# Linear attention and a channel mix on one core: batch 4 turned to tokens on partitions, all steps in a new order, 14 zero matmuls in front, the last tile in three pieces

## The chip, the core and the metric

The kernel runs on 1 core of one Trainium2 chip. The metric is the device time of one execution in microseconds (us): 198.37 us, the median of 3 runs (198.21 to 198.51). One more execution was taken with the profiler and is told apart below. The engines are TensorE (PE; its weight loads are PEld), VectorE (DVE), ScalarE (ACT), GpSimd (POOL) and SyncE (SP). POOL and SP issue the DMA transfers here.

## What is computed

```python
kv = np.einsum('bhsd,bhse->bhde', k, v)          # q, k, v: 8 batches, 8 heads, 576 tokens, 64
out = np.einsum('bhsd,bhde->bhse', q, kv)
rms = np.sqrt(np.mean(out * out, axis=-1, keepdims=True) + 1e-06)
x = (out / rms * g_norm)                         # then heads side by side: 8 x 576 x 512
x_prev = x shifted by one token, zero in front
xk = mu_k * x + (1 - mu_k) * x_prev              # xr likewise with mu_r
k = np.maximum(xk @ w_k, 0.0)                    # 512 -> 1024
v = k * k @ w_v                                  # 1024 -> 512
r = 1.0 / (1.0 + np.exp(-(xr @ w_r)))            # 512 -> 512
return r * v
```

Inputs and output are float32; the matmuls are in bfloat16.

## The kernel before

All eight batches are worked off in a pipeline. Nothing is scheduled by a compiler: ORDER (lines 18 to 109) is a list of words, and a loop at the end of the kernel issues one step for each word. `K.3.1.0=5` is step K of batch 3, part 1, half 0, into PSUM bank 5; a `'` at the end sends the step to VectorE instead of ScalarE. Each engine and each DMA queue gets its steps in the order of this list and works them off strictly in that order; semaphores make a step wait for its inputs and for a free buffer. A step at the head of a queue that waits holds up all behind it on that queue, and nothing on the others. So a place in the list says what a step is behind, and not when it runs.

**A batch a goes through these steps.** `ld.0.a`, `ld.1.a`, `ld.2.a` (line 201) load k, v and q on POOL's queue, with a cast to bfloat16. There are 3 buffers for k, 3 for v, 2 for q. `kv.a` (line 328) multiplies k and v on PE, 72 small matmuls into two banks; `kvo` copies them out. `qd.a.0` and `qd.a.1` (line 359) turn q on the DMA engines, issued by SP, into qT and qTr. `gt.a` (line 365) is a gate: POOL copies one column of qT, and so the loads listed behind it on POOL start only when qT has landed. Then u = q times kv in one of two forms:

- *Channels on partitions* (`u`, line 368): 24 matmuls of 64 x 64. `sq` squares on ScalarE, `ms` (line 436) averages over a head on PE by a matmul with a constant matrix, `rs` takes the reciprocal root on ScalarE, `mu` (line 448) scales on VectorE and writes xT. There are five pieces n = 0 to 4; the fifth holds the 64 tokens that are left over.
- *Tokens on partitions* (`ut`, line 386): 16 matmuls of 128 x 128 in four steps. `sqt` squares on ScalarE, `rdt` sums over a head on VectorE, `rst` takes the root of a small tile on ScalarE, `mut` scales on VectorE into y, `yd` (line 418) turns y into xT on the DMA engines, issued by SP, and `gs` (line 422) multiplies by g_norm on VectorE. Only the left-over 64 tokens go by `ur` (line 394) and one `sq`, `ms`, `rs`, `mu`; `kvr` (line 352) makes the operand of `ur`.

Before the change batches 2, 3 and 4 use the first form and 5, 6 and 7 the second; batches 0 and 1 have steps of their own at the start (`kc`, `qc`, `uc`, `Kf`, `Kl`).

With xT there, `d` (line 484) takes differences of neighbouring tokens, `sc` and `add` (lines 495, 508) blend them into xr (first index 1) and xk (0). `R` (line 572, 4 matmuls of 512 columns) and `S` make the sigmoid, `K` (line 552, 4 matmuls of 288 columns) is xk @ w_k, `Ko` its relu, `ks` its square, `V` (line 582, two halves of 4 matmuls) is the product with w_v. `fin` (line 597) multiplies V by the sigmoid into an out_sb tile (9 buffers) and `st` (line 613) stores it on SP's queue. A tile t of R and V has 128 tokens of a pair of batches, 0 to 8; t = 4 has 64 of each.

At the start `wm` (line 249) runs matmuls on zeros. The last tile is done apart: `L`, `Lf`, `Ls` (lines 588, 597, 619) in two column halves, each stored in two halves of 64 partitions, one on SP's queue and one on ScalarE's.

SP's queue has, between the start and the stage of batch 5, this order of transposes and stores (a store word of batches 0 and 1 is two transfers): qd.2.0, qd.3.0, qd.2.1, st.0.3, qd.3.1, st.0.0, st.0.1, qd.4.0, st.0.2, qd.4.1, st.1.5, st.1.6, qd.5.0, st.1.7, qd.5.1, st.1.8, st.2.1, st.1.4, qd.6.0, yd.5.0, yd.5.1, yd.5.3, yd.5.2, st.3.4, st.2.0, qd.7.0. POOL's queue has: (first loads), gt.2, gt.3, v3, k3, v4, k4, v5, q4, k5, gt.4, k6, q5, v6, gt.5, v7, k7, q6, q7, gt.6.

Of the kernel before, what the change touches and what calls it, by code (L numbers as in the profile page):

```python
# [18 lines left out]
    set.0 set.2 lraw.1 lraw.0 lrow wm.12=0 lf.0.2.0.2.0.576 lf.0.2.2.4.0.576 lf.0.0.2.3.0.576 lf.0.1.2.3.0.576  # L19
    set.1 wm.7=1 col.0=1 cast.1 cast.0' qc.0.0.2.192.576=23 qco.0.1.192.576 kc.0.0.2=45 kco.0.1 kco.0.0' wm.2=6  # L20
    uc.0.1=6 qc.0.2.4.0.192=70 qco.0.2.0.192' qco.0.3.0.192' qc.0.2.4.192.576=34 qco.0.0.192.576 sq.0.1 uc.0.0=5
    sq.0.0 col.1 qco.0.2.192.576' ms.0.1=2 rs.0.1 mu.0.1 qc.0.0.2.0.192=70 qco.0.0.0.192 ms.0.0=1 rs.0.0 mu.0.0
    kc.0.2.3=3 kco.0.2 wm.2=2 uc.0.2=2 sq.0.2 qco.0.3.192.576 lf.0.1.3.4.0.576 dc.0.0.2.256.576 lf.0.0.3.4.0.576
    kc.0.3.4=7 kco.0.3 wm.1=1 ms.0.2=1 rs.0.2 wm.1=6 uc.0.3=6 sq.0.3 uc.0.4=3 sq.0.4 sc.0.0.0.256.576'
    sc.0.0.1.256.576' qco.0.1.0.192' wm.1=5 uc.0.6=5 sq.0.6 add.0.0.0.256.576 mu.0.2 ms.0.3=4 rs.0.3 mu.0.3
    ms.0.4=7 rs.0.4 mu.0.4 wrap.0 uc.0.5=0 sq.0.5 ms.0.6=1 rs.0.6 dc.0.2.3.256.576 lf.1.2.0.4.0.576 wm.2=2
    qc.1.0.2.0.576=24 qco.1.1.0.576 qc.1.2.4.0.576=76 qco.1.3.0.576 fu.0.0.2.256.576 mu.0.6 dc.0.3.4.256.576
    ms.0.5=3 rs.0.5 qco.1.2.0.576 tab.1.0 fu.0.0.3.256.576 mu.0.5 dc.0.0.4.0.256 sc.0.0.0.0.256 sc.0.0.1.0.256
    lw.0.0.0.4.0.2 Kf.1.0.2.256=1 Kf.0.0.2.256=4 Kf.0.2.3.256 qco.1.0.0.576' lw.0.1.0.4.2.4 wm.2=6
    Kf.3.0.2.256=6 Kf.2.0.2.256=5 Kf.2.2.3.256 Kf.2.3.4.256 Kf.3.2.3.256 Kf.3.3.4.256 sc.0.1.0' sc.0.1.1'  # L30
# [24 lines left out]
    zl Ko.2.2.0' Ko.2.0.1' u.3.1=06 sq.3.2 sq.3.3 K.2.3.0=4 ks.2.0 K.2.1.0=3 Ko.2.3.0' st.1.6 K.2.5.1=7
    Ko.2.5.0' ms.3.3=1 K.2.1.1=5 rs.3.3 Ko.2.5.1' ms.3.2=4 rs.3.2 Ko.2.1.0' Ko.2.1.1' mu.3.2 ld.0.6 K.2.2.1=2
    ks.2.1 Ko.2.2.1 ld.2.5 u.3.2=7 kv.4=31 u.3.0=54 K.2.3.1=0 mu.3.3 K.2.6.1=2 kvo.4.3' ld.1.6 sq.3.4 kvo.4.2'
    qd.5.0 gt.5 kvo.4.0' sq.3.0 ms.3.0=6 sq.3.1 kvo.4.1' Ko.2.3.1 ks.2.5' rs.3.0 ks.2.2' K.2.7.1=1 ms.3.1=3
    rs.3.1 K.2.7.0=0 Ko.2.7.0 Ko.2.7.1' mu.3.0 K.2.4.1=6 K.2.6.0=1 ks.2.3' kvo.4.5 ks.2.7 mu.3.1 ms.3.4=3 rs.3.4
    Ko.2.6.0 K.2.4.0=0 Ko.2.4.0' Ko.2.4.1 ks.2.4 Ko.2.6.1 ks.2.6 d.3.0 d.3.4 mu.3.4 V.2.0.0=5 d.3.1 d.3.2  # L60
    V.2.3.0=4 sc.3.0.0' sc.3.1.0 sc.3.1.2 st.1.7 V.2.1.0=3 V.2.1.1 qd.5.1 kvo.4.4 sc.3.1.3' sc.3.0.3' sc.3.1.1
    sc.3.0.2 fin.2.1 st.1.8 st.2.1 add.3.1.1 V.2.0.1 fin.2.0 V.2.3.1 kv.5=10 kvo.5.3 kvo.5.0 u.4.1=62 u.4.0=73
    kvo.5.2 st.1.4 add.3.1.0 tab.1.3 R.3.7=5 sc.3.0.1' fin.2.3 kvo.5.1 R.3.6=0 S.3.6 sq.4.1 R.3.5=4 S.3.5 sq.4.2
    S.3.7 add.3.0.0 ld.1.7 ld.0.7 ld.2.6 R.3.4=1 S.3.4 add.3.0.1 K.3.3.0=0 R.3.8=4 S.3.8 tab.0.4 Ko.3.3.0'
    K.3.3.1=5 Ko.3.3.1' K.3.5.0=0 K.3.5.1=1 Ko.3.5.0' Ko.3.5.1' ms.4.1=4 rs.4.1 K.3.1.0=5 K.3.2.0=0 Ko.3.2.0'
    Ko.3.1.0 K.3.7.0=1 Ko.3.7.0' K.3.7.1=4 Ko.3.7.1' sq.4.3 sq.4.0 ms.4.2=5 rs.4.2 K.3.2.1=0 ms.4.3=1 K.3.6.0=4
    K.3.6.1=5 mu.4.1 Ko.3.2.1' ks.3.2' rs.4.3 mu.4.3 K.3.1.1=3 kvo.5.4 Ko.3.6.0' Ko.3.6.1 ks.3.6' Ko.3.1.1
    ks.3.7 ms.4.0=0 ld.2.7 K.3.4.0=1 mu.4.2 K.3.0.0=5 Ko.3.0.0 ks.3.1' ks.3.3 K.3.0.1=2 Ko.3.0.1 ks.3.0' rs.4.0
    mu.4.0 kvr.5.1' u.4.2=3 kv.6=45 kvo.6.3' sq.4.4 V.2.2.0=6 ks.3.5 Ko.3.4.0 V.2.2.1 d.4.0 kvo.5.5 fin.2.2
    ms.4.4=2 K.3.4.1=0 rs.4.4 mu.4.4 d.4.4 Ko.3.4.1 kvo.6.0 d.4.1 d.4.2 ks.3.4 d.4.3 sc.4.1.0 sc.4.0.0'  # L70
    V.3.6.0=7 sc.4.1.3' V.3.7.0=1 qd.6.0 gt.6 V.3.7.1 sc.4.1.1' fin.3.7 add.4.1.0 sc.4.1.2 sc.4.0.1 add.4.1.1
    kvo.6.1 V.3.5.0=2 ut.5.1=0 add.4.0.0 sc.4.0.2 V.3.6.1 fin.3.6 V.3.5.1 tab.1.4 sc.4.0.3' fin.3.5 R.4.1=6
    S.4.1 add.4.0.1 R.4.3=3 kvo.6.5 ut.5.0=1 sqt.5.0 rdt.5.0 kvr.6.0' R.4.0=4 S.4.0 S.4.3 sqt.5.1 rdt.5.1
    K.4.3.0=7 R.4.2=6 S.4.2 kvo.6.2 K.4.5.0=2 K.4.3.1=4 Ko.4.3.0' K.4.4.0=3 Ko.4.3.1' tab.0.5 kvr.5.0 Ko.4.5.0'
    ut.5.2=6 sqt.5.2 Ko.4.4.0' rst.5.0 mut.5.0 mut.5.1 yd.5.0 yd.5.1 K.4.5.1=5 K.4.2.0=7 rdt.5.2 kv.7=42
    ut.5.3=3 kvo.7.2' Ko.4.5.1 sqt.5.3 rdt.5.3 Ko.4.2.0 kvo.7.3 K.4.6.0=5 Ko.4.6.0' V.3.4.0=1 ks.4.3 rst.5.1
    mut.5.2 kvo.7.1 kvo.6.4 mut.5.3 K.4.4.1=0 V.3.4.1 fin.3.4 K.4.1.1=7 ur.5=2 kvr.6.1 Ko.4.4.1 sq.5.4 K.4.7.1=5
    K.4.7.0=6 K.4.2.1=0 Ko.4.7.0 ms.5.4=3 Ko.4.7.1 rs.5.4 Ko.4.2.1' mu.5.4 K.4.1.0=1 K.4.0.0=6 Ko.4.0.0
    K.4.0.1=5 ut.6.0=0 kvo.7.0' ks.4.5 Ko.4.0.1 ks.4.2 ks.4.0 sqt.6.0 Ko.4.1.0' ks.4.4 Ko.4.1.1' ks.4.1'
    K.4.6.1=3 Ko.4.6.1 ks.4.7' yd.5.3 gs.5.1 V.3.8.0=2 V.3.8.1 fin.3.8 ut.6.2=4 ks.4.6 V.4.1.0=6 ut.6.1=1  # L80
# [32 lines left out]
def kernel(  # L113
# [605 lines left out]
```

## Time and profile before

| | |
|---|---|
| runs shown | 198.37, 198.51, 198.21 us; median 198.37 |
| profiled execution, its own time | 198.81 us |
| its span, first to last instruction | 197.0 us |
| granted TensorE clock | 1.00 |
| last matmul starts and ends (line 593) | 191.13 for all 16; 193.06 us |
| kv.3, kv.4, kv.5, kv.6, kv.7 start on PE (line 337) | 66.75, 74.0, 84.57, 98.4, 114.04 us |

The profile page gives the busy time of each engine, then the span in 40 slices of 4.9 us, in which a digit is the busy share in tenths. The chain of waits gives who waited for whom. In a timeline the columns are start, duration, engine and line, operation, out<-in, count; the bracket holds the idle time before and what ended it. An answer on DMA issues gives the transfers issued in a window, the KB that each writes, and the median time from issue to landing. In a group of instructions the mean is that of one instruction; matmuls overlap, so the time that one takes on PE is read from a run of them: 64 K matmuls in 7.84 us (0.490 for a K), 20 V matmuls in 4.32 (0.864 for four), 16 R in 3.45, 72 kv in 0.71.

### The profile page before, as it was taken

The page shows a single profiled execution, that of the slowest core. Times are in us where ns is not written, and L with a number is a line of the kernel's source. Part 1 is how long each engine was busy: PE and PEld are TensorE (multiplying, and loading weights), DVE is VectorE, ACT ScalarE, POOL GpSimd, SP SyncE. Part 2 cuts the span into 40 slices and gives each one's busy share as a digit, 9 for nine tenths or more (in the row PEclk, how much of TensorE's full clock was granted, in tenths as well). Part 3 has the DMA queues.
Part 4 walks back from the last instruction along what each step waited for, and adds up shares of the span by engine and source line. Part 5 has one row for each costly group of instructions (what it writes and reads, how often), then busy time and mean ns, then how long its engine had stood idle before and what let it go on. Part 6 is the DMA issues. An engine that isn't in the chain of part 4 may idle for free.

```text
span 197.0 us, 4744 instructions
## 1 busy us (share of the span) xinstructions
PE 189.2 (96%) x1879; PEld 111.4 (57%) x1900; DVE 150.0 (76%) x331; ACT 153.4 (78%) x297; POOL 33.2 (17%) x54
## 2 busy tenths in 40 slices
PE   7989999999999999999999999999999999999991
PEld 2445754447744566456754667546854586476451
DVE  4177957894998778984989778897897898779141
ACT  3389799887688799999998978998699877267810
POOL 7864431000390000520090000000000000000000
PEclk9999999999999999999999999999999999999999
DMA  6999999999699999899979995982530426006053
GB/s 218 214 204 197 204 206 207 206 193 198 116 172 232 207 201 168 178 220 201 189 122 245 194 198 106 200 260 89 130 101 0 161 53 194 25 0 237 32 160 106
DMA packets 49035, 32.24 MB, mean 164 GB/s; under 512 B 25324, under 2 KB 44020, under 8 KB 49012
## 3 DMA queue, kind: packets, MB, share of 16 engines
q0 software_dynamic: 22160, 16.19, 54.9%
q1 hardware_dynamic: 26692, 15.61, 32.9%
q8 instruction: 15, 0.25, 0.5%
q10 hardware_dynamic: 160, 0.13, 0.3%
q14 instruction: 8, 0.07, 0.1%
HBM read 33.56 MB, written 9.44 MB: 218 GB/s over the span
## 4 chain that ended last, share of the span: by engine, by line
PE 85%; DVE 6%; ACT 6%; issue 1%; ACTq 0%
PE ps_v L585 28%; PE ps_km L555 24%; PE ps_r L575 15%; PE ps_warm L252 4%; PE ps_ms L438 3%; PE ps_km L530 2%; DVE xT L462 2%; PE ps_km L541 1%; PE ps_u L391 1%; PE ps_u L323 1%; ACT sq L434 1%; ACT L647 1%; ACT sig L580 1%; PE ps_kv L337 1%; PE ps_v L593 1%
## 5 line engine op out<-in xcount | busy, mean ns | idle before, releaser
L585 PE MATMUL ps_v<-wv_sb,sqk 128*128 128x512 bf16 x269 | 63.1, 379 | 0.5
L555 PE MATMUL ps_km<-xk,wk_sb 128*128 128x288 bf16 x448 | 61.0, 286 | 0.0
L555 PEld LDWEIGHTS <-wk_sb 128*128 128x128 bf16 x448 | 42.9, 98 | 14.7 <-issue 1.0
L585 PEld LDWEIGHTS <-sqk 128*128 128x128 bf16 x280 | 27.0, 98 | 30.5 <-ACT sqk L523 1.2
L519 DVE TENSOR_SCALAR rt<-ps_km 128x288 bf16<-128x288 f32 (+2 forms) x61 | 26.4, 460 | 10.1 <-PE ps_km L555 8.8
L575 PE MATMUL ps_r<-wr_sb,xr 128*128 128x512 bf16 x137 | 32.8, 379 | 0.5 <-DVE m L501 0.2
L600 DVE TENSOR_TENSOR out_sb<-ps_v,sig 128x512 f32<-128x512 f32 (+1 forms) x37 | 24.6, 671 | 10.0 <-PE ps_v L585 4.4
L517 ACT ACTIVATE rt<-ps_km 128x288 bf16<-128x288 f32 (+2 forms) x63 | 24.6, 419 | 8.8 <-PE ps_km L555 7.0
L499 ACT ACTIVATE m<-dx,cols 128x576 bf16<-128x576 bf16 (+1 forms) x32 | 22.4, 750 | 4.6 <-DVE dx L490 2.9
L580 ACT ACTIVATE sig<-ps_r 128x512 bf16<-128x512 f32 x36 | 20.7, 607 | 4.9 <-PE ps_r L575 4.6
L523 ACT ACTIVATE sqk<-rt 128x576 bf16<-128x576 bf16 (+1 forms) x33 | 22.3, 691 | 1.6 <-DVE rt L519 1.4
L575 PEld LDWEIGHTS <-xr 128*128 128x128 bf16 x144 | 14.0, 98 | 15.5 <-DVE xr L510 0.2
L462 DVE SCALAR_TENSOR_TENSOR xT<-ps_u,cols,rs 128x512 bf16<-128x512 f32 (+4 forms) x31 | 19.0, 626 | 3.7 <-ACT rs L443 3.4
L443 ACT ACTIVATE rs<-ps_ms,eps 128x512 f32<-128x512 f32 (+4 forms) x31 | 18.0, 593 | 3.9 <-PE ps_ms L438 3.6
L647 ACT ACT_TABLE_LOAD x15 | 19.2, 1283 | 0.3
L434 ACT ACTIVATE sq<-ps_u 128x512 bf16<-128x512 f32 (+4 forms) x31 | 14.6, 502 | 1.1 <-PE ps_u L323 1.0
L525 DVE TENSOR_TENSOR sqk<-rt 128x576 bf16<-128x576 bf16 (+2 forms) x27 | 12.9, 491 | 2.8 <-ACT rt L517 2.3
L366 POOL COPY gates<-qT 128x1 bf16<-128x1 bf16 x5 | 1.5, 305 | 74.1 <-DMA qT<-in_q 74.1
L510 DVE TENSOR_TENSOR xr<-m,xT 128x1152 bf16<-128x1152 bf16 x16 | 11.6, 752 | 1.6 <-ACT m L499 1.5
L510 DVE TENSOR_TENSOR xk<-m,xT 128x1152 bf16<-128x1152 bf16 (+2 forms) x17 | 11.7, 698 | 0.6 <-ACT m L499 0.5
L252 PE MATMUL ps_warm<-zeros 128*128 128x512 bf16 x27 | 10.0, 503 | 1.4 <-DVE eps L259 1.2
L501 DVE TENSOR_SCALAR m<-dx,cols 128x576 bf16<-128x576 bf16 (+2 forms) x34 | 10.9, 358 | 0.2
(80 smaller groups left out, 172.3 us busy)
## 6 DMA issues: line engine op xcount, KB each, us to landing
out_dram<-out_sb SPq DMA_DIRECT2D x23, 256.0 KB, 2.8
in_k<-in_k_dram POOLq DMA_DIRECT2D x7, 576.0 KB, 13.9
in_v<-in_v_dram POOLq DMA_DIRECT2D x6, 576.0 KB, 11.7
in_q<-in_q_dram POOLq DMA_DIRECT2D x6, 512.0 KB, 16.2
out_dram<-out_sb SPq DMA_DIRECT2D x24, 128.0 KB, 2.8
wk_sb<-in_moe_w_k_dram POOLq DMA_DIRECT2D x4, 256.0 KB, 10.6
wv_sb<-in_moe_w_v_dram POOLq DMA_DIRECT2D x2, 512.0 KB, 15.1
sqk<-in_v_dram SPq DMA_DIRECT2D x1, 576.0 KB, 3.7
```

The lines of the kernel that those rows point to most:

```text
L462: DVE.scalar_tensor_tensor(out=dst, in0=ps, scalar=g_sb, in1=rs, op0=ALU.mult, op1=ALU.mult)
L499: eng.activation(out=out_, in_=in_, func=AF.Copy, scale=mu)
L510: DVE.tensor_add(out=blended(a, which)[:, hs, c0:c1], in0=at[a]["m", which][:, hs, c0:c1], in1=xT[a % 2][:, hs, P + c0:P + c1])
L517: eng.activation(out=dst, in_=ps, func=AF.Relu)
L519: eng.tensor_scalar(out=dst, in0=ps, scalar1=0.0, scalar2=None, op0=ALU.max)
L523: eng.activation(out=dst, in_=src, func=AF.Square)
L555: nc.tensor.matmul(ps, wk_sb[:, cc, 128 * fc:128 * fc + 128], at[b]["xk"][:, cc, SH * h:SH * h + SH], start=(cc == 0), stop=(cc == NHP - 1))
L575: nc.tensor.matmul(ps, xr[:, cc, 128 * t:128 * t + 128], wr_sb[:, cc, :], start=(cc == 0), stop=(cc == NHP - 1))
L580: ACT.activation(out=sig[b, t], in_=give(("r", b, t)), func=AF.Sigmoid)
L585: nc.tensor.matmul(ps, sqk[:, fc, 128 * t:128 * t + 128], wv_sb[:, fc, :], start=(fc == 0), stop=(fc == NFC - 1))
L600: DVE.tensor_mul(out=o, in0=give(("v",) + key), in1=sig[b, t][:, c])
L647: "tab": lambda eng, n, b: ACT.preload_act_table_set(("abs_reciprocal_sqrt_and_small", "sigmoid_and_others")[n]),
```

## The change

ORDER is a new list throughout. Of the steps themselves:

- Batch 4 goes from `u` to `ut`: out go u.4.0 to u.4.2, four each of sq, ms, rs and mu; in come ut, sqt, rdt, mut and yd of 4.0 to 4.3, two each of rst, kvr and gs, and ur.4.
- The zero matmuls are 14 in front (12 and 7 before, around a wait for the small rows) and 27 in all instead of 30; kc.0 now stands ahead of the first qc.
- The last tile is done in pieces of 256, 128 and 128 columns, each stored by one transfer of 128 partitions: the first on SP, the second on ScalarE's queue, the third on SP.
- Some evacuations change between ScalarE and VectorE (Ko 55 and 57 before, 60 and 52 after; ks 32 and 24 before, 29 and 27 after).

SP's queue in the same stretch: qd.2.0, qd.3.0, qd.2.1, qd.3.1, st.0.2, st.0.0, st.0.1, qd.4.0, st.0.3, qd.4.1, st.1.5, st.1.7, qd.5.0, yd.4.1, yd.4.2, yd.4.3, yd.4.0, qd.6.0, st.1.6, qd.5.1, st.1.4, st.2.2, yd.5.1, yd.5.0, yd.5.3, yd.5.2, st.2.0, st.1.8, qd.7.0. POOL's queue: (first loads), gt.2, gt.3, v3, k3, v5, v4, k4, q4, k5, gt.4, k6, v6, q5, q6, gt.5, gt.6, k7, v7, q7. On PE, kv.6 now stands ahead of most of K.3, and kv.7 behind nine steps of K.4.

The diff, cut to what is spoken of:

```diff
-    set.0 set.2 lraw.1 lraw.0 lrow wm.12=0 lf.0.2.0.2.0.576 lf.0.2.2.4.0.576 lf.0.0.2.3.0.576 lf.0.1.2.3.0.576
-    set.1 wm.7=1 col.0=1 cast.1 cast.0' qc.0.0.2.192.576=23 qco.0.1.192.576 kc.0.0.2=45 kco.0.1 kco.0.0' wm.2=6
...
-    S.3.7 add.3.0.0 ld.1.7 ld.0.7 ld.2.6 R.3.4=1 S.3.4 add.3.0.1 K.3.3.0=0 R.3.8=4 S.3.8 tab.0.4 Ko.3.3.0'
...
-    mu.4.0 kvr.5.1' u.4.2=3 kv.6=45 kvo.6.3' sq.4.4 V.2.2.0=6 ks.3.5 Ko.3.4.0 V.2.2.1 d.4.0 kvo.5.5 fin.2.2
...
-    V.3.6.0=7 sc.4.1.3' V.3.7.0=1 qd.6.0 gt.6 V.3.7.1 sc.4.1.1' fin.3.7 add.4.1.0 sc.4.1.2 sc.4.0.1 add.4.1.1
...
-    ut.5.2=6 sqt.5.2 Ko.4.4.0' rst.5.0 mut.5.0 mut.5.1 yd.5.0 yd.5.1 K.4.5.1=5 K.4.2.0=7 rdt.5.2 kv.7=42
...
-    S.7.5 fin.7.5 st.7.5 fin.7.6 st.7.6 L.1=7 Lf.1 Ls.0.1 Ls.1.1 L.0=4 Lf.0 Ls.0.0 Ls.1.0
...
+    set.0 set.2 lraw.1 lraw.0 lrow wm.14=0 lf.0.2.0.2.0.576 lf.0.2.2.4.0.576 lf.0.0.2.3.0.576 lf.0.1.2.3.0.576
+    set.1 cast.1 cast.0' kc.0.0.2=12 kco.0.0 qc.0.0.2.0.192=34 qco.0.1.0.192' kco.0.1' qc.0.0.2.192.576=56
...
+    sqt.4.3 fin.2.0 sc.3.0.1 R.3.7=2 V.2.3.1 S.3.7 qd.5.0 ut.4.1=0 gt.5 R.3.6=3 sqt.4.1 kvo.5.5' kvr.4.0
...
+    tab.0.4 rst.4.0 K.3.4.0=2 Ko.3.4.0' ut.4.2=3 K.3.4.1=6 Ko.3.4.1' mut.4.0 mut.4.1 kv.6=41 kvo.6.0 kvr.5.1'
+    yd.4.1 kvo.6.1 sqt.4.2 rdt.4.2 ks.3.4 K.3.6.1=2 K.3.5.0=6 K.3.3.0=4 K.3.5.1=5 Ko.3.5.0 Ko.3.5.1 K.3.6.0=0
+    K.3.1.1=6 Ko.3.6.0 rdt.4.3 Ko.3.3.0 K.3.1.0=5 kvr.4.1 kvo.6.3' rst.4.1 mut.4.2 mut.4.3 yd.4.2 yd.4.3
+    Ko.3.6.1 ks.3.6' Ko.3.1.0 Ko.3.1.1' K.3.2.0=0 Ko.3.2.0 K.3.3.1=4 Ko.3.3.1 ur.4=2 kvo.6.2' kvo.6.4' yd.4.0
...
+    K.3.7.1=5 kvo.6.5 sq.4.4 ut.5.2=6 Ko.3.2.1' ks.3.0' ks.3.2 Ko.3.7.1' ms.4.4=3 rs.4.4 fin.2.2 qd.6.0 gs.4.1
...
+    sc.4.1.1' gt.6 add.4.1.0 V.3.4.0=0 sc.4.1.2 V.3.5.0=7 qd.5.1 ut.5.0=5 st.1.4 add.4.1.1 sqt.5.0 kvr.5.0
+    sc.4.0.0 st.2.2 ld.0.7 V.3.7.0=3 V.3.7.1 V.3.5.1 ld.1.7 fin.3.7 sc.4.0.3 V.3.6.0=4 V.3.6.1 fin.3.6 fin.3.5
...
+    K.4.2.1=1 K.4.4.0=0 yd.5.0 Ko.4.5.0 Ko.4.5.1' rdt.5.3 rst.5.1 Ko.4.1.1' mut.5.2 mut.5.3 yd.5.3 kv.7=73
...
+    V.7.5.1 fin.7.5 V.7.7.0=4 st.7.5 V.7.7.1 S.7.7 fin.7.7 st.7.7 L.1=2 Lf.1 Ls.0.1 L.0=1 Lf.0 Ls.1.0 L.2=5
+    Lf.2' Ls.0.2
...
+    LAST = (slice(0, C // 4), slice(C // 2, C), slice(C // 4, C // 2))
+
     def last_vv(part):
 
-        c = slice(C // 2 * part, C // 2 * part + C // 2)
+        c = LAST[part]
         ps = take(("v", B - 1, 8, part), [128, c.stop - c.start], FP32, "ps_v")
         for fc in range(NFC):
             nc.tensor.matmul(ps, sqk[:, fc, 128 * 8:128 * 8 + 128], wv_sb[:, fc, c], start=(fc == 0), stop=(fc == NFC - 1))
@@ -595,7 +598,7 @@
     outs = {}
 
     def finish(b, t, part=None):
-        key, c = (b, t) if part is None else (b, t, part), slice(0, C) if part is None else slice(C // 2 * part, C // 2 * part + C // 2)
+        key, c = (b, t) if part is None else (b, t, part), slice(0, C) if part is None else LAST[part]
         o = outs[key] = work.tile([128, c.stop - c.start], FP32, tag="out", name="out_sb", bufs=9)
         DVE.tensor_mul(out=o, in0=give(("v",) + key), in1=sig[b, t][:, c])
 
@@ -611,16 +614,15 @@
         return ((slice(0, 128), rows_.rearrange("(p t) c -> t p c", t=4)[(0, 2, 1, 3)[t if t < 4 else t - 5]]),)
 
     def store(b, t, part=None, queue=0):
-        key, c = (b, t) if part is None else (b, t, part), slice(0, C) if part is None else slice(C // 2 * part, C // 2 * part + C // 2)
+        key, c = (b, t) if part is None else (b, t, part), slice(0, C) if part is None else LAST[part]
         o = outs.pop(key)
         for n, (ps_, dst) in enumerate(rows_of(b, t)):
             (nc.sync, nc.scalar)[queue].dma_start(out=dst[:, c], in_=o[ps_])
 
-    def store_half(n, part):
+    def store_last(n, part):
         o = outs[B - 1, 8, part]
         dst = rows_of(B - 1, 8)[0][1]
-        c = slice(C // 2 * part, C // 2 * part + C // 2)
-        (nc.sync, nc.scalar)[n].dma_start(out=dst[half(n), c], in_=o[half(n)])
+        (nc.sync, nc.scalar)[n].dma_start(out=dst[:, LAST[part]], in_=o)
 
     ops = {
         "set": lambda eng, n: setup(n),
@@ -679,7 +681,7 @@
         "st": lambda eng, b, t, *n: store(b, t, None, *n),
         "L": lambda eng, part: last_vv(part),
         "Lf": lambda eng, part: finish(B - 1, 8, part),
-        "Ls": lambda eng, n, part: store_half(n, part),
+        "Ls": lambda eng, n, part: store_last(n, part),
     }
 
     for word in ORDER.split():
```

## The prediction

> **What bounds the kernel now.** First the page: busy times and the slices.
>
> ```profile
> PE 189.2 (96%) x1879; PEld 111.4 (57%) x1900; DVE 150.0 (76%) x331; ACT 153.4 (78%) x297; POOL 33.2 (17%) x54
> PE   7989999999999999999999999999999999999991
> DMA  6999999999699999899979995982530426006053
> ```
>
> TensorE (PE) is full from the second slice to the last, so the order of its list sets the time, and a cut of its work counts in full, unless something it needs is late. The DMA engines are just as full until about 115 us, so "something late" can be a load. Next I read who waits on the queues: POOL (loads) and SP (transposes, stores).
>
> ```profile
> POOL gates L366 <- DMA qT<-in_q: 74.1, 5, 21.8
> ```
>
> ```profile
> SPq L361 <- DMA in_q<-in_q_dram: 79.5, 4, 39.6
> ```
>
> Both issue in list order. POOL stands 74.1 us in five gates, each until a batch's transposed q (qT) has landed; SP stands 79.5 us at four q transposes, each until its q has landed. Whatever is listed behind them on that queue stands too. So I read both queues in order of time.
>
> ```profile
> 80.71 0.48 POOL L366 COPY gates<-qT 128x1 bf16<-128x1 bf16 x1 [21.79 <-DMA qT<-in_q]
> 81.22 0.74 POOL L199 DMA_DIRECT2D in_k<-in_k_dram  x1
> 82.34 1.03 POOL L211 DMA_DIRECT2D in_q<-in_q_dram  x1 [0.37 <-issue]
> 83.36 0.69 POOL L213 DMA_DIRECT2D in_qr<-in_q_dram  x1
> 84.04 0.78 POOL L199 DMA_DIRECT2D in_v<-in_v_dram  x1
> 98.09 0.19 POOL L366 COPY gates<-qT 128x1 bf16<-128x1 bf16 x1 [13.28 <-DMA qT<-in_q]
> ```
>
> ```profile
> 92.11 3.45 SPq L361 DMA_TRANSPOSE qT<-in_q  x1
> ...
> 113.32 3.30 SPq L361 DMA_TRANSPOSE qT<-in_q  x1
> 116.72 5.67 SPq L420 DMA_TRANSPOSE xT<-y  x4
> 122.49 1.81 SPq L617 DMA_DIRECT2D out_dram<-out_sb  x3
> ```
>
> One loop is visible: gate 4 opens at 80.7, k6, q5, v6 are issued, SP takes up q5's transpose at 92.1, gate 5 opens at 98.1 and lets k7 and v7 go. The answers on DMA issues give times to landing: k6 8.1, q5 9.6, v6 11.7 us, so 89.3, 91.9 and 95.7; v7 9.0 and k7 11.2 after 98.58 and 99.31, so 107.6 and 110.5. Loads land in queue order, one 576 KB load each 2.8 to 3.5 us, a q (512 KB) 2.6. kv.7 needs k7 and v7 and runs on PE at 114.04, 3.5 us after them; kv.6 runs at 98.4, 2.7 us after v6.
>
> **The change, part by part.** *PE work.* Batch 4 loses u.4.* (16 matmuls in 0.56, 8 in 0.20) and four of its five ms (0.216 each): 1.62 us. It gains 16 ut (0.22 per four) and ur (0.12): 1.01. Net -0.6, all in the full stretch.
>
> *ScalarE, VectorE.* VectorE gains 4 rdt at 0.678, 4 mut at 0.685, 2 gs at 0.480 and loses 4 mu at 0.746: +3.4 us. ScalarE loses 4 sq and 4 rs (0.601, 0.689), gains 4 sqt (0.590), 2 rst (0.303), 2 kvr (0.40): -1.4. VectorE is busy 10.6 of the 15 us from 85 to 100, so its 4.4 idle us cover it: nothing taken; 3.4 us if that cover were gone. Other steps change engine (5 Ko go to ScalarE, 3 ks to VectorE); both have 40 us free in the span: nothing, within 1 us.
>
> *Front.* 27 zero matmuls instead of 30, kc ahead of qc. All this lies before kc.1, whose second half needs v1's second part: issued at 16.12, landing in 13.2, so 29.3, and PE is there at about 29.4 today. The bytes ahead of it on the queue are the same, as is the PE work ahead. Taken: 0 (0 to 0.1 us gained; had PE been later than the load, it would lose the difference).
>
> *Loads earlier needed.* The load list after gate 3 puts v5 ahead of v4 and k4; the seventh and last is k5, 58.09 + 21.0 = 79.1, the same seven transfers, hence the same time. kv.3 needs k3 (53.61 + 9.7 = 63.3), then 15.3 us of PE work lead to kv.5, which the new list reaches at 78.6: kv.5 starts at 79.1 (84.6 now). The new order has used up the lead that loads had over PE.
>
> *The loop, moved.* After gate 4 the order is now k6, v6, q5, q6. v6 takes q5's place (89.3 + 2.9 = 92.2), q5 comes at 92.2 + 2.6 = 94.8 (bounds: 91.9, its landing today; 95.7, today's third place). kv.6 is 12.1 us of PE work after kv.5 (11 V halves and R at 0.864, 4 ut at 0.22, 2 K at 0.49, kv 0.71): 91.2, so it waits 1.0 for v6.
> On SP the four yd.4 are now behind qd.5.0 and ahead of qd.6.0. SP idles until 94.8, then needs qd.5.0 and four yd: 113.32 to 122.49 in the fence above, 9.1 us (bounds 7.4: a qT issue at 124.47 took 2.33 and four yd at 159.35 5.13; and 9.2). So qd.6.0 starts at 103.9 (q6 is long there).
> yd.4.0 starts at 102.7, lands 2.5 later, 105.2; from the last gs to the xr add behind it took 4.4 us in batch 5 (124.84 to 129.20): R.4 can start at 109.6. PE gets there 16.2 us after kv.6, 108.4: another wait of 1.2.
> qT6 lands 5.4 to 6.8 after qd.6.0 (six rows, middle 6.0): gate 6 opens at 109.9. And **k7 and v7 are now behind gate 6**, not gate 5. From gate to the second 576 KB landing: gate 3 10.9 (52.44 to 63.3), gate 4 11.5 (k6 plus one step), gate 5 12.4 (98.09 to 110.5); middle 11.6. kv.7 can start at 109.9 + 11.6 = 121.5. PE's own work puts it 25.2 after kv.6 plus the 1.2 at R.4: 118.6. It waits 2.9 us, with no PE work listed that could pass it.
>
> *Rest.* From kv.7 the new list has 55 K, 36 V halves, 14 R, 8 ut, 3 ur, 3 ms, kv and the L pieces: 75.2 us. Today the stretch from 114.04 to the last matmul's end at 193.06 is 79.0 for 78.4 of listed work; the same 0.6 of small gaps is added: 121.5 + 75.8 = 197.3, today 193.06.
>
> *Tail.* Today 3.94 us from there to the span's end. The last VectorE piece has 128 columns: 512 take 0.685, 256 take 0.424, so 0.29 instead of 0.42. The L pieces of 128 columns have no row at this line; the ut matmuls (128 columns) take 0.056 each, the 256-column L 0.12: taken 0.056, worst 0.9 us more. One 64 KB store instead of two on two queues (2.2 and 2.5): 0. Tail 3.8, span 201.1, 4.1 above 197.0. The profiled execution took 198.81, 0.44 above the median 198.37; I move the median by the same 4.1: **202.5 us**.
>
> **One rule against this.** The Trainium skill, page "DMA: Bandwidth & Descriptors", section "Anatomy of one DMA — SWDGE (gpsimd) path", gives a DMA as about 2.0 us plus its bytes over 436 GB/s. By it (an estimate) k7 and v7, 1152 KB each in float32, would land about 7.5 us after their issue, and the wait would be gone. The rows here say 6.9 to 9.0 for the first load alone, under stores and transposes, so the trace doesn't agree; it is the side of rival C.
>
> **Rivals.** *B, smaller:* the chain is at its short bounds (91.9 + 7.4 + 5.4 + 10.9 = 115.6), so k7 and v7 are there before PE, but the waits at kv.6 or R.4 remain: kv.7 at up to 118.6 instead of 121.5, **199.6** and down to no change. For it: three of four terms have a shorter row. Against: all must be short together.
> *C, faster:* the loads after the gates land in the time that the nearest lone load shows (sqk from in_k at the start, 4.6, then 2.6 to 2.9 per load). Then v6 is there at 88.7, q5 at 91.3, gate 6 opens by 104.1 and kv.7's loads land by 112; PE runs through, kv.7 at 79.1 + 12.1 + 25.2 = 116.4, 5.1 earlier: **197.4**. It decides wherever gate 6 opens before about 105. Against: each batch behind a gate took 6.9 or more.
> *D, slower still:* all long bounds, 95.7 + 9.2 + 6.8 + 12.4 = 124.1: 205.1; beyond that the SP stores queued behind qd.6.0 hold up out_sb tiles (nine of them) and with them VectorE.
>
> **Chances.** Forecast (200.2 to 205.1) 0.60; B 0.15, of which 0.05 falls within 0.2% (198.0 to 198.8) and 0.10 above; C (196.7 to 197.9) 0.20; D above 205.1 0.05. Faster 0.20, same 0.05, slower 0.75; 0.2% is about what a measurement of this kernel can tell from no change. The range from 197.6 to 205.1 leaves out D and most of C, under 0.2.
>
> **What would show it.** On PE (weight loads included) a wait of 1.5 to 5 us at L337 for in_k or in_v near 120, with gate 6 at 108 to 111; SP at qd.5.0 until about 95, and the four yd.4 (L420) directly behind it; smaller waits at kv.6 near 92 and R.4 near 109. Wrong if gate 6 opens before 105, if yd.4 are issued before 92, or if kv.7 starts without a wait. The front is right if kc.1's second half starts at 29.3 to 29.8; the tail if the span ends 3.6 to 4.0 us after the last matmul.

## The result, and the profile after

The changed kernel takes **202.24 us** (median of 6 runs, 201.44 to 202.67), the kernel before 198.38 (198.21 to 198.92, 6 runs beside them). The ratio is 1.0179, 95% interval 1.0161 to 1.0197: slower, by 3.2 to 3.9 us. The forecast was 202.5. The profiled execution took 201.94 us with a span of 200.2 at a granted clock of 1.0.

First the page: busy times and the slices.

```profile
PE 189.9 (95%) x1897; PEld 111.3 (56%) x1897; DVE 156.0 (78%) x345; ACT 149.2 (75%) x290; POOL 33.1 (17%) x54
PE   7999999999999998999998979999999999999992
DMA  6999999999699999799968899895220326254053
```

A slice is 5.0 us here. PE has an 8 in the slice from 105 us and a 7 in the one from 115, where it had nines. The time went there: kv.3, kv.4, kv.5, kv.6 start at 62.98, 73.35, 78.58, 91.92, and kv.7 at 121.04, 7 us later than before (114.04), although kv.6 is 6.5 us earlier. From kv.7 to the end of the last matmul (196.27) nothing is lost. Now the two queues, POOL first, in order of time.

```profile
80.25 0.19 POOL L367 COPY gates<-qT 128x1 bf16<-128x1 bf16 x1 [22.56 <-DMA qT<-in_q]
...
81.88 0.76 POOL L200 DMA_DIRECT2D in_v<-in_v_dram  x1 [0.37 <-issue]
82.63 0.89 POOL L212 DMA_DIRECT2D in_q<-in_q_dram  x1
...
109.15 0.76 POOL L367 COPY gates<-qT 128x1 bf16<-128x1 bf16 x1 [6.94 <-DMA qT<-in_q]
109.85 0.76 POOL L200 DMA_DIRECT2D in_k<-in_k_dram  x1
110.59 0.76 POOL L200 DMA_DIRECT2D in_v<-in_v_dram  x1
```

```profile
94.67 3.88 SPq L362 DMA_TRANSPOSE qT<-in_q  x1
98.64 6.04 SPq L421 DMA_TRANSPOSE xT<-y  x4
104.85 1.92 SPq L362 DMA_TRANSPOSE qT<-in_q  x1
106.81 1.66 SPq L620 DMA_DIRECT2D out_dram<-out_sb  x2
108.57 1.20 SPq L364 DMA_TRANSPOSE qTr<-in_qr  x1
109.82 1.87 SPq L620 DMA_DIRECT2D out_dram<-out_sb  x3
```

This is the loop of the prediction, step by step: q5 lands at 94.5 (issue 82.63, 11.9 to landing), qd.5.0 goes out, the four yd.4 (L421) follow, qd.6.0 starts at 104.85, gate 6 opens at 109.15, and k7 and v7 go out behind it. They land 6.9 and 9.9 us after their issue: v7 at 120.5. Now PE's waits from 60 us on (total, times, longest), and the chain of waits in order of time.

```profile
PE ps_km L556 <- DVE out_sb L603: 1.4, 1, 1.4
PE ps_r L576 <- DVE xr L511: 1.1, 2, 0.9
PE ps_v L586 <- ACT rt L518: 0.5, 1, 0.5
PE ps_kv L338 <- DMA in_k<-in_k_dram: 0.4, 1, 0.4
PE ps_kv L338 <- DMA in_v<-in_v_dram: 0.3, 1, 0.3
PE ps_u L392 <- DMA qT<-in_q: 0.3, 1, 0.3
```

```profile
109.82 0.59 SPq L620
110.41 0.04 issue
110.45 6.69 DMA out_dram<-out_sb
...
117.26 0.70 DVE out_sb L603
117.97 0.04 issue
118.01 3.10 PE ps_km L556 x24
121.11 0.71 PE ps_kv L338 x72
```

Here the trace differs from the forecast: the wait behind 117 us isn't at kv.7 but at the K steps just ahead of it. VectorE stood at fin.3.4 for an out_sb tile, because the store that frees it, st.1.4, stood on SP behind all those transposes, went out at 109.82, and took 6.69 us to land beside the loads of k7 and v7. VectorE held back a copy of K.4, and PE its next K. When PE came to kv.7 at 121.04, v7 had been there for half a microsecond.

### The profile page after: what moved, and what is told of

It reads as the page before. It is cut to its first block, busy times and chain, and to the rows that moved or that the text cites. A ratio compares the mean times of both kernels' runs of the same rounds, so it can differ in the third digit from the quotient of the medians.

```text
span 200.2 us, 4769 instructions
## 1 busy us (share of the span) xinstructions
PE 189.9 (95%) x1897; PEld 111.3 (56%) x1897; DVE 156.0 (78%) x345; ACT 149.2 (75%) x290; POOL 33.1 (17%) x54
## 4 chain that ended last, share of the span: by engine, by line
PE 66%; issue 13%; DMA 8%; SPq 4%; ACT 3%; POOL 2%; DVE 1%; DVEq 0%; POOLq 0%; ACTq 0%
PE ps_km L556 22%; PE ps_v L586 19%; PE ps_r L576 10%; DMA in_v<-in_v_dram 5%; PE ps_warm L253 4%; DMA out_dram<-out_sb 3%; PE ps_km L531 2%; PE ps_ms L439 2%; SPq L421 2%; PE ps_km L542 1%; POOL in_k L200 1%; SPq L620 1%; PE ps_kv L338 1%; ACT sq L435 1%; SPq L362 1%
## 5 line engine op out<-in xcount | busy, mean ns | idle before, releaser
L586 PE MATMUL ps_v<-wv_sb,sqk 128*128 128x512 bf16 x280 | 64.6, 379 | 0.5 <-ACT rt L518 0.5
L576 PE MATMUL ps_r<-wr_sb,xr 128*128 128x512 bf16 x144 | 33.7, 379 | 1.1 <-DVE xr L511 1.1
L603 DVE TENSOR_TENSOR out_sb<-ps_v,sig 128x512 f32<-128x512 f32 (+2 forms) x38 | 24.1, 657 | 13.3 <-PE ps_v L586 7.2
L518 ACT ACTIVATE rt<-ps_km 128x288 bf16<-128x288 f32 (+1 forms) x64 | 24.4, 415 | 10.0 <-PE ps_km L556 8.7
L581 ACT ACTIVATE sig<-ps_r 128x512 bf16<-128x512 f32 x36 | 20.2, 596 | 10.7 <-PE ps_r L576 10.5
L524 ACT ACTIVATE sqk<-rt 128x576 bf16<-128x576 bf16 (+1 forms) x30 | 20.5, 694 | 1.6 <-DVE rt L520 1.3
L463 DVE SCALAR_TENSOR_TENSOR xT<-ps_u,cols,rs 128x512 bf16<-128x512 f32 (+4 forms) x27 | 16.0, 608 | 3.0 <-ACT rs L444 2.9
L526 DVE TENSOR_TENSOR sqk<-rt 128x576 bf16<-128x576 bf16 (+2 forms) x30 | 14.3, 486 | 3.0 <-ACT rt L518 2.4
L444 ACT ACTIVATE rs<-ps_ms,eps 128x512 f32<-128x512 f32 (+4 forms) x27 | 15.0, 585 | 1.7 <-PE ps_ms L439 1.5
L435 ACT ACTIVATE sq<-ps_u 128x512 bf16<-128x512 f32 (+4 forms) x27 | 12.3, 496 | 1.9 <-PE ps_u L324 1.4
L502 DVE TENSOR_SCALAR m<-dx,cols 128x576 bf16<-128x576 bf16 (+2 forms) x34 | 11.3, 367 | 0.3
L417 DVE TENSOR_TENSOR y<-ps_u,rst 128x512 bf16<-128x512 f32 x16 | 10.4, 685 | 1.0 <-ACT rst L410 1.0
## 6 DMA issues: line engine op xcount, KB each, us to landing
in_v<-in_v_dram POOLq DMA_DIRECT2D x6, 576.0 KB, 11.3
```

Source lines behind the costliest of these rows:

```text
L463: DVE.scalar_tensor_tensor(out=dst, in0=ps, scalar=g_sb, in1=rs, op0=ALU.mult, op1=ALU.mult)
L518: eng.activation(out=dst, in_=ps, func=AF.Relu)
L524: eng.activation(out=dst, in_=src, func=AF.Square)
L576: nc.tensor.matmul(ps, xr[:, cc, 128 * t:128 * t + 128], wr_sb[:, cc, :], start=(cc == 0), stop=(cc == NHP - 1))
L581: ACT.activation(out=sig[b, t], in_=give(("r", b, t)), func=AF.Sigmoid)
L586: nc.tensor.matmul(ps, sqk[:, fc, 128 * t:128 * t + 128], wv_sb[:, fc, :], start=(fc == 0), stop=(fc == NFC - 1))
```

## The experiments

Three theories. **Q**: the chain of the prediction, with the landing of k7 and v7 as its end. **S**: the same chain on SP, but with the store of an out_sb tile as its end. **V**, the rival: VectorE's extra 3.4 us and the new order itself. A fourth, **C** (contention of transposes and loads), came out of the first run. Ratios are against the kernel before (198.6 to 198.8 in these runs); the changed kernel has 1.0179.

### 1. Loads ahead of gate 6

```diff
-... qd.5.0 ut.4.1=0 gt.5 R.3.6=3 ... st.2.2 ld.0.7 V.3.7.0=3 V.3.7.1 V.3.5.1 ld.1.7 fin.3.7
+... qd.5.0 ut.4.1=0 gt.5 ld.0.7 ld.1.7 R.3.6=3 ... st.2.2 V.3.7.0=3 V.3.7.1 V.3.5.1 fin.3.7
```

> The changed kernel with the loads of k7 and v7 listed ahead of gate 6 (right behind gate 5), nothing else. In the profile of the changed kernel two holds end together at kv.7: PE stands 1.39 us at K.4 (118.01) because VectorE waits for an out_sb tile, and v7 lands at 120.5, 0.5 us before PE reaches kv.7 at 121.04. Theory Q (what the prediction said: k7 and v7 behind gate 6): the loads go out at 102 to 104, land by about 113, and the store that took 6.69 us to land beside them lands in the 2.8 us of the other stores, so that the hold at K.4 goes too: kv.7 at about 119.6, 1.4 us gained, 200.8. Theory S (the store st.1.4 comes too late on SP, whatever runs beside it): K.4 still starts near 118 and nothing is gained, 202.2. Theory V (the new order and VectorE's extra 3.4 us are what costs): 202.2, with VectorE's own work ending the wait at K.4. A rival inside Q: loads at 102 run beside the four yd.4 and qd.6.0 and make R.4 later, 202.2 to 204.

Measured: 210.56 us, 1.0603 (1.0567 to 1.0638), 8.3 us **slower** than the changed kernel. The rival inside Q was right, and much larger than priced. From the chain of waits of this run:

```profile
102.64 1.26 SPq L416
103.90 0.05 issue
103.95 10.27 DMA xT<-y
...
118.03 5.55 PE ps_r L571 x16
```

The last yd.4 takes 10.27 us to land beside k7 and v7 (4.0 in the changed kernel, where these two loads aren't out yet), and R.4, which needs it, starts at 118.03 instead of 109.92. SP itself is held: qd.6.0 takes 7.50 us to issue instead of 1.92.

```profile
106.32 7.50 SPq L357 DMA_TRANSPOSE qT<-in_q  x1
```

So gate 6 isn't just a delay that the change put on k7 and v7; it keeps their loads off the y transposes. As a second loss, R.4 then takes 5.55 us for its 16 matmuls instead of 3.45 to 3.62. The windows of this run show why (after the stretch its length, the busy times of PE, PEld, DVE, ACT and POOL with their counts, then PEclk, DMA share, GB/s):

```profile
109.00:118.00 9.00, 0.53 (x3) 0.04 (x1) 4.03 (x12) 1.48 (x3) 1.16 (x2) 0.65 1.08 172
118.00:120.00 2.00, 1.97 (x5) 0.63 (x6) 2.00 (x4) 2.00 (x5) 0.69 (x1) 0.50 0.57 69
120.00:122.00 2.00, 2.00 (x6) 0.76 (x5) 1.90 (x4) 1.09 (x3) 0.00 (x0) 0.51 1.16 236
122.00:124.00 2.00, 2.00 (x11) 0.88 (x9) 1.55 (x3) 1.73 (x4) 0.00 (x0) 1.00 1.49 204
```

While PE stood, the granted clock (0.65, 0.50, 0.51, 1.00) fell to half, and for 4 us after it worked at half speed.

### 2. Stores ahead of qd.5.0, and both moves

```diff
-... V.2.3.1 S.3.7 qd.5.0 ...
+... V.2.3.1 S.3.7 st.1.6 st.1.4 qd.5.0 ...
```

> The changed kernel with the stores st.1.6 and st.1.4 listed ahead of qd.5.0 on SP, where SP idles from 84.4 to 94.7, nothing else. Theory S: VectorE has its out_sb tile at 115.4, the 1.39 us at K.4 go, PE reaches kv.7 at 119.6 and then waits for v7, which lands at 120.5 as before: 0.5 us gained, 201.7, with a wait of about 0.9 at kv.7 for in_v in place of the one at K.4. Theory Q: the same, since the load stands right behind; less if the bytes of the stores delay v6 and q5 (256 KB each, some 1 us): 202 to 203. Theory V: 202.2, the wait at K.4 stays.

Measured: 202.41 us, 1.0191 (1.0167 to 1.0215), no change. The hold at K.4 is gone (VectorE waits for no out_sb tile), but the four store transfers run beside v6 and q5 in the stretch where the DMA engines are full: kv.6 now waits 2.30 us for in_v (0.33 before), qd.5.0 starts at 96.87, and kv.7 runs at 121.59. The clause on bytes was the right one: moved traffic was paid for at the place that it was moved to.

> The changed kernel with both moves: k7 and v7 ahead of gate 6, st.1.6 and st.1.4 ahead of qd.5.0. If the two holds near kv.7 are the whole of it (Q and S together): no wait at K.4 or kv.7, 1.4 us gained against the changed kernel, 200.8, and with the small waits at R.4 (0.91), kv.6 (0.33) and ut.5 (0.27) still there it stays above the kernel before (198.4). If the SP chain alone set R.4 and all behind it, R.4's wait grows and less is gained: 201.5. Theory V: 202.2.

Both together: 210.62 us, 1.0588 (1.0551 to 1.0624), as the first move alone. R.4 waits 8.66 us, its last transpose takes 10.54 to land. Neither Q nor S foresaw it; C does.

### 3. Without the four transposes

Two runs leave out yd.4.0 to yd.4.3, with the loads ahead of gate 6 as in the first run, and with the loads where the change has them.

```diff
-    yd.4.1 kvo.6.1 sqt.4.2 rdt.4.2 ks.3.4
+    kvo.6.1 sqt.4.2 rdt.4.2 ks.3.4
...
-    rst.4.1 mut.4.2 mut.4.3 yd.4.2 yd.4.3 Ko.3.6.1
+    rst.4.1 mut.4.2 mut.4.3 Ko.3.6.1
...
-    kvo.6.2' kvo.6.4' yd.4.0 K.3.0.0=5
+    kvo.6.2' kvo.6.4' K.3.0.0=5
```

> The run with k7 and v7 ahead of gate 6 (210.6) once more, without the four yd.4: batch 4's 512 turned tokens are left as they stand in xT, all other work is done. It asks whether the 8.5 us at R.4 came from those four transposes being beside the loads. Theory C: yes, then nothing is left for R.4 to wait for, and the order runs to its end at the speed of PE: 197.5 to 200. If the loads beside qd.6.0 or the stores hold up something else (out_sb tiles behind qd.6.0's long issue): 201 to 206 with VectorE waiting for out_dram. If the 8.5 us had another cause: near 210.

> The changed kernel without the four yd.4 (batch 4's 512 turned tokens are left as they stand in xT); k7 and v7 stay behind gate 6. It parts the two halves of the prediction's step: the four transposes ahead of qd.6.0, and the place of k7 and v7 behind gate 6. If the four transposes make the delay: qd.6.0 goes out at 98.6, gate 6 opens near 104.5, v7 lands by 116, before PE gets to kv.7 at 117.5 to 118.4, and the time is that of the run without them and with the loads ahead, 198.8. If the place of the loads costs by itself: kv.7 waits for in_v to 120 or more, 201.

Measured: 198.80 us (1.0011, 0.9982 to 1.0040) and 198.86 us (1.0018, 0.9998 to 1.0037). These are the runs that settle the cause: with the four transposes the loss goes, but for 0.7 us at most (the upper end, 1.0037). Once they are out, it makes no difference whether k7 and v7 stand behind gate 5 or gate 6; with them in, it made 8.3 us. The runs show the sum of what the transposes do, not its parts: without them R.4 doesn't wait for batch 4 either (0.91 and 0.18 us in the changed kernel). POOL and PE of the second:

```profile
103.98 0.30 POOL L362 COPY gates<-qT 128x1 bf16<-128x1 bf16 x1 [1.51 <-DMA qT<-in_q]
104.22 0.76 POOL L195 DMA_DIRECT2D in_k<-in_k_dram  x1
104.97 0.76 POOL L195 DMA_DIRECT2D in_v<-in_v_dram  x1
```

```profile
114.64 3.59 PE L551 MATMUL ps_km<-xk,wk_sb 128*128 128x288 bf16 x28
118.16 0.78 PE L333 MATMUL ps_kv<-in_v,in_k 64*64 64x64 bf16 x72
```

Gate 6 opens 5.2 us sooner, v7 lands at 114.7 (9.7 after its issue), st.1.4 goes out at 104.6, and PE runs into kv.7 at 118.16 with no bracket behind either line. V falls: all of VectorE's added work is still there.

### 4. A later gate, and the stores on another queue

A new step gy.4 lets POOL copy a column of xT that yd.4.0 writes, and k7 and v7 follow it instead of gate 6. The other edit sends two stores from ScalarE's queue.

```diff
-... ur.4=2 kvo.6.2' kvo.6.4' yd.4.0 K.3.0.0=5 ...
+... ur.4=2 kvo.6.2' kvo.6.4' yd.4.0 gy.4 ld.0.7 ld.1.7 K.3.0.0=5 ...
```

```diff
-... gs.4.1 mu.4.4 st.1.6 gs.4.0 ... ut.5.0=5 st.1.4 add.4.1.1 ...
+... yd.4.0 st.1.6.1 st.1.4.1 K.3.0.0=5 ... gs.4.1 mu.4.4 gs.4.0 ... ut.5.0=5 add.4.1.1 ...
```

> The changed kernel with k7 and v7 held back by a new gate instead of gate 6: POOL copies one column of xT that yd.4.0 writes, and they follow it; q7 stays behind gate 6. Theory C (contention, formed on the run with both loads ahead of gate 6, where yd.4.0 took 10.3 us to land instead of 3.1 to 4.0): the loads go out at 105.5 instead of 109.9, no yd.4 is in flight any more, R.4 starts at 109.9 as in the changed kernel, v7 lands near 116 and kv.7 waits for nothing. But qd.6.0 now runs beside the loads, takes some 7 us of SP instead of 1.9, and the store st.1.4 behind it goes out at 115 instead of 109.8, so VectorE waits for its out_sb tile until 118 to 120 and K.4 starts 1 to 3 us later: 203 to 205. If SP isn't held up: kv.7 at 119.6 and 200.8. Theory Q (only the landing of k7 and v7 counts): 200.8.

Measured: 205.08 us, 1.0337 (1.0295 to 1.0379), at the upper end of what C and S gave, though by another store than the one named: SP was not held (qd.6.0 took 1.85), but st.1.6 landed late. R.4 starts at 109.92 as before, so no transpose of y was hurt. From the chain of waits and PE's timeline:

```profile
107.85 7.49 DMA out_dram<-out_sb
```

```profile
116.17 1.86 PE L574 MATMUL ps_r<-wr_sb,xr 128*128 128x512 bf16 x4 [2.97 <-DVE out_sb L601]
```

The wait at the out_sb tile came sooner and was longer. And k7 and v7, issued 3.4 us earlier, gained little by it: k7 landed at 115.3 instead of 116.8, and v7 at 120.0, 12.8 us after its issue, instead of 120.5, 9.9 after it. So an earlier start moved the end of v7 by half a microsecond only. That the traffic of qd.6.0 and the stores beside them is the reason is likely, but no run shows it.

> The changed kernel with st.1.6 and st.1.4 taken from SP's queue to ScalarE's, listed right behind yd.4.0, so that they go out at about 97 to 101, where the DMA engines are least busy. Theory S: VectorE's wait for the out_sb tile goes, and so do the 1.39 us at K.4; kv.7 then waits for v7, which lands at 120.5 or, with two stores fewer beside it, up to 1 us sooner. SP gets to qd.5.1 1.7 us sooner. 201.2 to 201.7, with K.4 unheld. ScalarE pays four issues, some 2 us, in a stretch where it is busy 14.4 of 18 us: no cost expected. If the stores slow the yd.4 transposes instead, as loads did: R.4 later by 1 to 2, 202.5 to 203.5.

Measured: 204.04 us, 1.0257 (1.0198 to 1.0315). Slower than S gave; the interval, 202.7 to 205.0 us, reaches into what the other outcome gave (202.5 to 203.5), but not by its way, a later R.4. The wait for an out_sb tile is gone, as S said, but ScalarE paid for it:

```profile
99.21 4.72 ACTq L615 DMA_DIRECT2D out_dram<-out_sb  x3
103.98 0.71 ACT L513 ACTIVATE rt<-ps_km 128x288 bf16<-128x288 f32 x2 [4.67 <-DMA xT<-y]
```

ScalarE stood 4.67 us at its stores, by the profile until a yd.4 had landed. PE then waited 1.84 and 1.67 us for ScalarE, and the granted clock was 0.50 from 107 to 109. This run doesn't test S cleanly, since it put a new wait on another engine.

> Both: k7 and v7 behind the new gate on yd.4.0, and st.1.6 and st.1.4 on ScalarE's queue behind yd.4.0. Theories C and S together say that this is the order that takes both holds away without a load beside a yd.4 transpose: no wait at K.4, none at kv.7, kv.7 at 119.6 or a little before, 200.8 (1.4 less than the changed kernel). What is left above the kernel before are the waits at R.4 (0.9), kv.6 and the V behind ks. If another thing is late behind these two: 202.

Measured: 204.30 us, 1.0282 (1.0246 to 1.0318): the same two waits at ScalarE (2.13 and 1.67). A miss, for the same reason.

### 5. S alone, and slack on PE

Ten out_sb buffers instead of nine take that wait away without moving a transfer. The last run also moves kv.7 back in PE's list.

```diff
-        o = outs[key] = work.tile([128, c.stop - c.start], FP32, tag="out", name="out_sb", bufs=9)
+        o = outs[key] = work.tile([128, c.stop - c.start], FP32, tag="out", name="out_sb", bufs=10)
```

```diff
-... yd.5.3 kv.7=73 kvo.7.3 K.4.2.0=2 ... kvo.7.0 ur.5=5 sq.5.4 K.4.0.0=6 ... K.4.0.1=1 ks.4.5 ...
+... yd.5.3 K.4.2.0=2 ... ur.5=5 sq.5.4 K.4.0.0=6 ... K.4.0.1=1 kv.7=73 kvo.7.3 kvo.7.0 ks.4.5 ...
```

> The changed kernel with 10 out_sb buffers instead of 9 (room for it comes from laying the zero tile over kv_heads[1] and the small rows over xr, both long before those are used); no transfer and no step moves. VectorE's fin.3.4 then takes the buffer of st.1.6, issued 1.7 to 3 us before st.1.4. Theory S: the 1.39 us at K.4 go, PE reaches kv.7 at 119.6 and waits there for v7, which still lands at 120.5: a wait of 0.9 for in_v at kv.7, 0.4 gained, 201.8. If st.1.6 lands as late as st.1.4 did: nothing, 202.2. If the store was the only hold: 200.8.

Measured: a ratio of 1.0148 (1.0107 to 1.0190), 201.6 us by 1.0148 x 198.64; the profiled execution took 201.02. The intervals overlap with that of the changed kernel, so the time alone decides nothing, but the trace does:

```profile
120.00 0.91 PE L334 MATMUL ps_kv<-in_v,in_k 64*64 64x64 bf16 x72 [0.37 <-DMA in_v<-in_v_dram]
```

The wait at K.4 is gone and kv.7 waits for v7, as S expected: two holds of nearly the same end, one behind the other.

> Ten out_sb buffers, and kv.7 with its two first evacuations moved behind K.4.0.1 in the list, past four halves of K.4 and ur.5 (2.1 us of PE work). If the two holds (out_sb, and v7 landing at 120.5) are all there is between 114 and 122, PE works through them: kv.7 without a wait at about 121.7, 1.4 us gained against the changed kernel, 200.8. If another thing is late behind them (evacuations of ut.5 or K.4, yd.5 and the R.5 that needs it): 201.3 to 202.2, with the wait showing there.

Measured: 201.99 us, 1.0163 (1.0135 to 1.0192). kv.7 runs without a wait at 122.07, and the next wait comes at once:

```profile
124.38 0.65 PE L552 MATMUL ps_km<-xk,wk_sb 128*128 128x288 bf16 x4 [0.82 <-ACT kvh L241]
```

A K half needs a PSUM bank that kv.7 has just filled and ScalarE copies out. The 1.4 us expected didn't come; the bank order is tied to the place of kv.7.

> The changed kernel with three zero matmuls more at about 22 us (wm.1 ahead of Kf.7 becomes wm.4), some 0.41 us each, so 1.2 us more of PE work ahead of everything that follows. If the transfers set the times of kv.3 to kv.7 (gates, loads, transposes, none of which waits for PE before 98 us), PE only eats into its own waits, 3.4 us in all between kv.3 and kv.7 in the changed kernel: 202.2 to 202.6. If PE sets the time: 1.2 us more, 203.4. The prediction's step on the front (a gain or loss there is swallowed by a load) stands with the first.

Measured: 202.23 us, 1.0169 (1.0142 to 1.0197), as the changed kernel. PE is 1.1 us later at kv.3 (64.08), kv.4 and kv.5, and on time again at R.4:

```profile
93.11 0.77 PE L333 MATMUL ps_kv<-in_v,in_k 64*64 64x64 bf16 x72 [0.41 <-DMA in_v<-in_v_dram]
...
117.98 3.10 PE L551 MATMUL ps_km<-xk,wk_sb 128*128 128x288 bf16 x24 [1.27 <-DVE out_sb L598]
121.01 0.78 PE L333 MATMUL ps_kv<-in_v,in_k 64*64 64x64 bf16 x72
```

The edit was priced too high: four zeros took 1.08 us (21.42 to 22.50) where one took 0.43, so it added 0.65 us and not 1.2. V.0 started at 33.34 instead of 31.93; the other 0.76 us came from the start of this execution, where PE waited 1.11 us at 7.96 for VectorE behind a later first load, with the same list up to there. So PE was 1.4 us late, 0.65 of it by the edit, and all but 0.1 of it was gone at R.4 (110.02, 109.92 in the changed kernel). Up to kv.7 PE doesn't set the time of the changed kernel for a delay of this size.

### 6. The tail alone, on the kernel before

```diff
-    S.7.5 fin.7.5 st.7.5 fin.7.6 st.7.6 L.1=7 Lf.1 Ls.0.1 Ls.1.1 L.0=4 Lf.0 Ls.0.0 Ls.1.0
+    S.7.5 fin.7.5 st.7.5 fin.7.6 st.7.6 L.1=7 Lf.1 Ls.0.1 L.0=4 Lf.0 Ls.1.0 L.2=3
+    Lf.2' Ls.0.2
```

> The kernel before with the new tail alone: the last tile in pieces of 256, 128 and 128 columns, each stored by one transfer of 128 partitions. The prediction's term: the last VectorE piece 0.29 instead of 0.42 us, the L matmuls at 0.056 per 128 columns cost nothing more, 198.2 (0.1 less than before). Rival: the 128-column matmuls cost as much as 256-column ones, 0.9 us more: 199.2. A second rival: one store of 128 partitions lands later than two halves on two queues, 0.3 us more: 198.5.

Measured: 198.21 us against 198.66, 0.9976 (0.9959 to 0.9994): 0.1 to 0.8 us faster, and the only version here that beats both kernels. The L matmuls cost the same cut finer:

```profile
190.98 1.93 PE L596 MATMUL ps_v<-wv_sb,sqk 128*128 128x256 bf16 x24
```

24 of them in 1.93 us, where 16 took 1.91. Both rivals fall.

## Why the prediction was right, point by point

| Step | Predicted | Changed kernel | Without yd.4 |
|---|---|---|---|
| kv.5 starts | 79.1 | 78.58 | 78.83 |
| v6, q5 land | 92.2, 94.8 | 91.8, 94.5 | |
| kv.6 waits | 1.0 | 0.33 | 0.31 |
| qd.6.0 starts | 103.9 | 104.85 | |
| gate 6 opens | 109.9 | 109.15 | 103.98 |
| R.4 can start | 109.6 | 109.92 | 109.12, no wait |
| v7 landed | 121.5 | 120.5 | 114.7 |
| kv.7 starts | 121.5 | 121.04 | 118.16 |
| last matmul ends | 197.3 | 196.27 | 193.40 |

*The loop held, with errors that cancel.* From the start of qd.5.0, just behind q5's landing, to qd.6.0 took 10.2 us, over the upper bound of 9.2: qd.5.0 took 3.88 and four yd.4 6.04, and the gaps did the rest. Not all of the 6.04 is issue time: in it SP waited for VectorE's work on batch 4.

```profile
SPq L421 <- DVE sqk L526: 1.3, 1, 1.3
SPq L421 <- DVE rt L520: 1.1, 1, 1.1
```

qT6 landed in 4.3 us, under the lower bound of 5.4, with no load in flight (q6 had landed at 98.2). Gate to v7's landing took 11.3 (11.6).

*The last releaser failed.* The prediction let kv.7 wait 2.9 us for v7. In its place 1.39 us were lost at K.4, to the store behind qd.6.0 that rival D named, and kv.7 waited for nothing. D let this mechanism in only beyond 205.1; in fact it was level with the loads already at 121. With the buffer added, the wait is at kv.7 and is 0.37. That kv.7 would start without a wait was one of the prediction's own signs of being wrong, and here it did. The place came out because both hang on the same queue. That the sum came out to half a microsecond (121.5, measured 121.04) is luck in part: PE's own time was put 1.05 us too low, and the last wait was put at 2.9 and measured 1.39.

*PE's own time to kv.7 was short.* It was put at 118.6; without the K.4 wait it is 121.04 - 1.39 = 119.65. Without yd.4 and with the loads ahead, kv.6 to kv.7 took 25.5 us for 25.2 listed, and kv.5 to kv.6, less 1.1 of waits, 12.5 for 12.1.

*"k7 and v7 are now behind gate 6" is a link, and not a cost of its own.* As a link of the chain it is right. But the two runs without yd.4 show that the gate costs nothing by itself, and the first run shows that without it the kernel would be slower still. What costs are four more DMA transposes in the stretch where qd.5.0, qd.6.0, two stores and the next loads have to pass.

*Front:* no time was gained or lost there, as forecast, and by the mechanism forecast. kc.1's second half starts at 29.1, right behind v1's second part, which landed at 29.04 (issued at 15.74, 13.3 to landing); the sign asked for 29.3 to 29.8 and was missed by 0.2. PE is at V.0 0.64 us sooner than in the profile before (31.93, before 32.57), but most of that isn't the change: the other executions with the new front have V.0 between 31.90 and 32.46 (the run with three more zeros aside), and the other one with the old front has 32.33. At kv.3 PE waits 0.37 us for k3. The run with three more zeros says that a delay of 1.4 us is swallowed as well.

*PE work -0.6, VectorE +3.4:* VectorE's busy time rose by 6.0 us (150.0 to 156.0) and ScalarE's fell by 4.2 (153.4 to 149.2). Evacuations at the front had changed sides too, which the prediction didn't count. That was free all the same, as the runs without yd.4 show, which keep it. PE's saving wasn't seen as time: the second of these runs still holds 1.4 us of small waits (0.5 + 0.3 + 0.3 + 0.3). Taken off, they would leave 197.5, near the 197.4 of rival C; that is arithmetic, and no run had it. C's condition, gate 6 open before about 105, is met there (103.98), but not by C's way: gate to v7's landing still took 10.7 us.

*Rest and tail:* kv.7 to the last matmul's end took 75.2 us (75.8 predicted), the tail 3.9 (3.8).

*The rule* of the Trainium skill (page "DMA: Bandwidth & Descriptors", section "Anatomy of one DMA — SWDGE (gpsimd) path") gave an estimate of 7.5 us for k7 and v7 together. They took 10.7, from 109.85 to 120.5. The trace doesn't agree, as the rows of before said.

*Open:* how much of the 3.4 us between the changed kernel and the run without yd.4 is SP's time and how much is traffic on the DMA engines. The edits that part the two moved a wait elsewhere each time. SP's waits for VectorE in the four yd.4 (1.3 and 1.1 us) and R.4's for batch 4 (0.91 and 0.18) are further parts that no run takes off alone.

## What to carry to other kernels

- When a step is traded for one that uses the DMA engines (here a transpose for four squares and four root steps), price its place on the queue: what stands behind it on SP moves back, the stores and, through transposes and gates, the loads. Here that cost 3.4 us, and the PE work saved elsewhere didn't show.
- Before moving a load ahead of a gate, look at what the gate keeps it away from.
- When one chain holds up several things at once, taking off the last one may only uncover the next (here with a wait of 0.37 us, and then of 0.82). Look for what they share.

## What the runs showed of the hardware that was not expected

- In the two runs with k7 and v7 issued ahead of gate 6, the transposes were slowed far more than the loads: yd.4.0 landed in 10.27 and 10.54 us, in 4.0 in the changed kernel, where those loads were not out yet, and SP took 7.50 and 8.15 us to issue qd.6.0, not 1.92. In the first of them v7 went from 9.9 to 10.7 us. Not every load does that much: the yd.5 landed in 3.1 to 3.8 us with q7's load still in flight, and in 4.6 to 6.0 beside v7 and q7 in the two runs with ten buffers.
- A store sent from ScalarE held that engine for 4.67 us, by the profile until a transpose sent from SP had landed (4.96 us in the run with both moves). Why it waits wasn't tried.
- The granted clock fell to 0.50 after PE had stood 8.5 us, after 2.97 us, and after 1.84 and 1.67 us (or 2.13 and 1.67) close together, and stayed there for 2 to 6 us; after 1.39 us alone and after 2.30 us alone it stayed at 1.00. The Trainium skill, page "TensorE: Matmul & The Clock Gate", section "What's actually happening", gives half rate after an idle window of about 3.4 us. The stand of 8.5 us agrees. The one of 2.97 is shorter than that, and the pairs of short ones, with PE busy 0.89 of 4 us (103 to 107 us) in the first, show that the gap needn't be in one piece.
